# Scores of every second key tile in two borrowed banks, weight conversions in pairs, and a new order on every engine

## Chip, core and metric

The kernel runs on one core of one Trainium2 chip. The metric is the device time of one execution in microseconds; the figure given for a kernel is the median of its timed runs. The core has TensorE (PE) for matrix products, VectorE (DVE), ScalarE (ACT) and GpSimd (POOL) for elementwise work, SyncE (SP), which issues all the DMA transfers here, and 16 DMA engines. PSUM has 8 banks of 128 x 512 fp32.

## The reference

Block-sparse attention of 4 batches x 8 heads, 768 positions and head size 64, and behind it a feed-forward layer of 3072 tokens, 512 to 2048 to 512, with `h - tanh(h)` between:

```python
scores = scale * np.matmul(q, k.transpose(0, 1, 3, 2))
...
scores = np.where(mask, scores, -1000000000.0)
scores = scores - np.max(scores, axis=-1, keepdims=True)
attn = np.exp(scores)
attn = attn / (np.sum(attn, axis=-1, keepdims=True) + 1e-09)
return np.matmul(attn, v).astype(np.float32)
...
h = x @ w_in
g = h - np.tanh(h)
return (g @ w_out).astype(np.float32)
```

The mask lets each block of 32 queries see its neighbours, the first and last block and three sampled blocks.

## The kernel before

**Tiles and steps.** Heads come in pairs that are loaded together (`load_qk`, `load_v`). Queries and keys are split into a high part (`high`, ACT, L333) and a low part (`low`, L339), which are copied by DMA (`dist`, L362) into the slab: slots A and B for the maxima and the first half of the scores, C and D for the cross terms. The mask rides along as extra rows of A and B (`fill`). A step is one head and two of its six key tiles, so there are 96 steps, three per head. In step s, for key tile x of 0 and 1:

- `scores(s, x)`: four matmuls (L488, L489) into `pst`, 128 keys x 768 queries, two banks
- `expo(s, x)`: ACT's exponential (L492) from `pst` to `pe`
- `p_high` (ACT, L498) and `p_low` (POOL, L507): P as the sum of two fp16 parts, `ph` and `pl`
- `accum(s)`: 36 matmuls (L521, L524, L525) of P with V into `pav`

The maximum of each query row has to be known before its scores are exponentiated. It is found two heads ahead: `smax` (L455) writes score tiles to `psm` (three banks), `maxima` (DVE, L461) reduces two of them, `turn_max`, `neg_max` (L473) and `put_max` (a DMA of 3 KB, L479) put the row into slot B. V gets a scale (`v_max` L417, `v_all` L425, `v_scale` L429) and two fp16 parts (`v_high` L438, `v_low` L442). `norm` divides, `spill` writes the result out.

**Banks.** `pst` 2, `psm` 3, `pav` 1, and the two feed-forward banks `bank0` and `bank1`. In the first 28 steps these two serve only the start and the conversion of eight weight tiles: a tile is staged (`stage_w`), put together from its 64-bit words by three DVE operations (`convert`, L751, L755, L759) in a bank, and split into a high part (`res_hi`, ACT, L815) and a low part (`res_lo`, DVE, L819). `WSTEP` gives the step of each.

**Feed-forward.** From step 28 on pieces of four token chunks are worked on between the steps (`h_part` L854, `g_part`, `o_part`). What remains comes behind the last step: all its PE products are of 512 columns. Behind the attention its PSUM tiles are given to the feed-forward (`pf`).

**Order.** Each operation is added to a plan with a due time, an engine, a duration, and what it reads and writes. Sorted by due time, the operations of each engine are then taken in the order that the table `ORDER` says: each character is how many places ahead in the list of what is left the next one stands. So the due times and the table together fix one order for each engine, and an engine never leaves it. From durations and hops the plan works out a start for each operation; these starts set in which order the program text is emitted, and the count of fillers: `KeepBusy` puts small products of ones into `pav` (L240) where PE's plan has a gap.

Of the kernel before, what the change touches and what calls it, by code (L numbers as in the profile page):

```python
# [11 lines left out]
F32 = mybir.dt.float32  # L12
F32R = mybir.dt.float32r
F16 = mybir.dt.float16
# [30 lines left out]
        "#$$#'##$#############$##$#&$$###(%$###$#%$###$#$$$#$#%##'###%%%#&###%%$##%##$$##%##$$###%%###%#&$%$###&&###$#%"
        "#$#%$#######$######$##$#&$$$$###$##########'##$###$########'''#&#$##%&$$##&&#(%'#&*$###&'%%#&&#$$#%$%'##%%$#'&"
        ")%$&&#(##&#(#%$#$$&##$#&%%'##%%$#$$%$&#&%'#$&#$$#%#$''#$#$##%&#$&$%###$$''$$&##&*'#%$%##'$%($###$('#$$###$$('$"
        "$&#&&*#$#%$##'&$#''#*$#%&##('##)%($#%$#&#%$&#%($'#%#$#$%##'%$&$'#$##'$#)##&%##'###(%$$'(##%)#&&$'##&$)'#%'#(#$"
        "$#%'#'%$##%)&#%'#$#%%)(#$)###&*$#'$&$#'$%#'#&#)#'###''#)%($&#$('%%#%#%#$#%%$$(&#$'##&#$#'$'#$###$$'#%)$#&###%#"
        "#$(%#%$#'#*$'%##%##&%##$$$#$#%#$$##"  # L50
    ),
    "ACT": (
        "###$##$$$%$&%&%#,##%##$&#$#0#%##$#$#%3##$#$#$#$#$#$#%##$#$#,###$#$#1$#$#$#$#$#'#####%##,%$%$##%$#########'##$#"
        "####$####%$#$#%$%$%$%$%$%###$$$##$#%##$##$#$#$#$%$#$&#$#%##&#$#$#$*####%##$#%$#%$%$#$#$$#'##$$$#($#%$#%$%#####"
        "$#$#2#'#%$##$#$$$#&$$###%$%$###$#$#$#$#$#'#%###$#$$#&$#####$###$#$$$#$&#$####$#&#$#$##(#%###$#%$#%##%$#$#))##'"
        "#*$#(##$#$%$###%####$#$4#$$###$###$#$$#%#$$##$%$#$#$###$#####$#%##+#%#######'&$$#$#$#$$###%$$#1%#%####&%#%##($"
# [1096 lines left out]
```

## Time and profile before

| | us |
|---|---|
| median of 3 timed runs | 922.56 (921.46 to 923.68) |
| profiled execution | 921.18 |
| its span, first to last instruction | 919.4 |
| PE busy | 895.2 (97%) |
| DVE busy | 701.5 (76%) |
| ACT busy | 654.0 (71%) |
| POOL busy | 485.4 (53%) |

The busy shares are means over two very different parts. The attention, with pieces of feed-forward in it, lasts to about 463 us; behind it is feed-forward alone. PE's busy time is modelled (matmuls are pipelined) and in the early part holds the fillers. "Releaser" or "<-" in a row names what ended an engine's idle time.

### The profile page before, as it was taken

The page shows a single profiled execution, that of the slowest core. Times are in us where ns is not written, and L with a number is a line of the kernel's source. Part 1 is how long each engine was busy: PE and PEld are TensorE (multiplying, and loading weights), DVE is VectorE, ACT ScalarE, POOL GpSimd, SP SyncE. Part 2 cuts the span into 40 slices and gives each one's busy share as a digit, 9 for nine tenths or more (in the row PEclk, how much of TensorE's full clock was granted, in tenths as well). Part 3 has the DMA queues.
Part 4 walks back from the last instruction along what each step waited for, and adds up shares of the span by engine and source line. Part 5 has one row for each costly group of instructions (what it writes and reads, how often), then busy time and mean ns, then how long its engine had stood idle before and what let it go on. Part 6 is the DMA issues. An engine that isn't in the chain of part 4 may idle for free.

```text
span 919.4 us, 18275 instructions
## 1 busy us (share of the span) xinstructions
PE 895.2 (97%) x7177; PEld 744.8 (81%) x7177; DVE 701.5 (76%) x1000; ACT 654.0 (71%) x964; POOL 485.4 (53%) x324
## 2 busy tenths in 40 slices
PE   8998999999999999999989999999999999999998
PEld 4777778888887888888878888888888888888886
DVE  6987878889887888886469999985667666765765
ACT  5888888988889798798865666665555555555553
POOL 5677887778777676778842434532212222222131
PEclk9999999999999999999999999999999999999999
DMA  8878588766878758465352333230014202300201
GB/s 228 205 187 240 133 219 225 206 174 178 208 233 193 199 134 278 109 168 178 94 162 92 104 92 94 90 115 1 1 70 155 86 24 92 127 23 1 92 1 46
DMA packets 57677, 120.73 MB, mean 131 GB/s; under 512 B 6170, under 2 KB 26836, under 8 KB 56568
## 3 DMA queue, kind: packets, MB, share of 16 engines
q1 hardware_dynamic: 57592, 119.58, 45.5%
q8 instruction: 56, 0.92, 0.4%
q14 instruction: 29, 0.24, 0.1%
HBM read 55.68 MB, written 26.21 MB: 89 GB/s over the span
## 4 chain that ended last, share of the span: by engine, by line
PE 84%; ACT 6%; DVE 4%; DMA 3%; issue 2%; SPq 1%; POOL 0%; ACTq 0%; DVEq 0%
PE bank L854 27%; PE pf L889 8%; PE pf L891 8%; PE pf L890 8%; PE pst L488 7%; PE pst L489 6%; PE psm L455 5%; PE pav L521 3%; PE pav L524 3%; PE pav L525 3%; ACT pe L492 3%; PE bank L889 1%; DMA raw<-qk 1%; PE bank L890 1%; PE bank L891 1%
## 5 line engine op out<-in xcount | busy, mean ns | idle before, releaser
L507 POOL TENSOR_TENSOR pl<-pe,ph 128x768 f16<-128x768 f32 x192 | 320.4, 1688 | 95.4 <-ACT ph L498 49.8
L884 POOL TENSOR_TENSOR gl<-t,gh 128x512 fp32r<-128x512 f32 x96 | 126.9, 1323 | 298.6 <-ACT gh L882 233.3
L492 ACT ACTIVATE pe<-pst 128x768 f32<-128x768 f32 x192 | 155.2, 808 | 54.1 <-PE pst L489 52.1
L461 DVE TENSOR_REDUCE mc<-psm 128x2 f32<-128x1536 f32 x93 | 163.0, 1753 | 30.5 <-PE psm L455 29.8
L498 ACT ACTIVATE ph<-pe 128x768 f16<-128x768 f32 x192 | 157.9, 840 | 2.7 <-PE pav L525 0.3
L488 PE MATMUL pst<-slab 128*128 128x512 f32 (+1 forms) x384 | 141.6, 369 | 8.7 <-ACT pe L492 7.4
L868 DVE TENSOR_TENSOR t<-t,bank 128x512 f32<-128x512 f32 x96 | 65.7, 684 | 94.3 <-ACT t L866 69.0
L489 PE MATMUL pst<-slab 97*128 97x512 f32 (+1 forms) x384 | 122.4, 340 | 0.0
L521 PE MATMUL pav<-vhl,ph 128*128 128x65 f16 x1152 | 116.4, 194 | 0.1
L524 PE MATMUL pav<-vhl,ph 128*128 128x64 f16 x1152 | 115.8, 195 | 0.0
L525 PE MATMUL pav<-vhl,pl 128*128 128x65 f16 x1152 | 115.3, 192 | 0.0
L521 PEld LDWEIGHTS <-ph 128*128 128x128 f16 x1152 | 105.5, 96 | 7.0 <-issue 4.4
L874 ACT ACTIVATE u<-u,bias 128x512 f32<-128x512 f32 x96 | 69.2, 721 | 58.3 <-DVE bank L876 57.8
L524 PEld LDWEIGHTS <-ph 128*128 128x128 f16 x1152 | 106.6, 97 | 0.4 <-issue 0.2
L525 PEld LDWEIGHTS <-pl 128*128 128x128 f16 x1152 | 106.7, 99 | 0.0
L488 PEld LDWEIGHTS pst<-slab 128*128 128x128 f32 x384 | 72.6, 189 | 32.0 <-ACT pe L492 19.7
L455 PE MATMUL psm<-slab 88*128 88x512 f32 (+1 forms) x378 | 87.9, 350 | 5.9 <-DVE nm L473 1.9
L866 ACT ACTIVATE t<-bank 128x512 f32<-128x512 f32 x96 | 56.7, 591 | 43.5 <-PE bank L854 38.8
L864 ACT ACTIVATE u<-bank 128x512 f32<-128x512 f32 x96 | 57.0, 594 | 43.0 <-PE bank L854 41.8
L882 ACT ACTIVATE gh<-t 128x512 fp32r<-128x512 f32 x96 | 60.3, 628 | 36.3 <-DVE t L880 18.1
L880 DVE COPY_PREDICATED t<-u,bank 128x512 f32<-128x512 int32 x96 | 71.5, 745 | 18.9 <-ACT u L874 13.5
L890 PE MATMUL pf<-wx,gh 128*128 128x512 f32 x216 | 84.1, 389 | 0.0
(135 smaller groups left out, 1918.5 us busy)
## 6 DMA issues: line engine op xcount, KB each, us to landing
slab<-hm SPq DMA_DIRECT2D x124, 192.0 KB
slab<-lo SPq DMA_DIRECT2D x63, 192.0 KB
raw<-qk SPq DMA_DIRECT2D x15, 768.0 KB
stage<-w_in SPq DMA_DIRECT2D x16, 512.0 KB
stage<-w_out SPq DMA_DIRECT2D x16, 512.0 KB
xsav<-xbuf SPq DMA_DIRECT2D x4, 2048.0 KB
rawv<-v SPq DMA_DIRECT2D x16, 384.0 KB
xscr<-xq SPq DMA_DIRECT2D x16, 384.0 KB
```

The costliest lines, as they stand in the source:

```text
L455: nc.tensor.matmul(o[:, b0 + c0 : b0 + c1], lhsT=sB[s][0:88, t * P : (t + 1) * P], rhs=sA[s][0:88, c0:c1], start=True, stop=True)
L461: nc.vector.tensor_reduce(out=mcs[h][:, t - 1 : t + 1], in_=psm.rearrange("p (x s) -> p x s", x=2), op=ALU.max, axis=AX.X)
L488: nc.tensor.matmul(pst[:, q], lhsT=sC[c][:, kc], rhs=sD[c][:, q], start=True, stop=False)
L489: nc.tensor.matmul(pst[:, q], lhsT=sA[a][0:97, kc], rhs=sB[a][0:97, q], start=False, stop=True)
L492: nc.scalar.activation(out=pe[s % 2][:, x * S : (x + 1) * S], in_=pst[:, 0:S], func=AF.Exp, scale=0.125)
L498: nc.scalar.activation(out=phs[s][0][:, c], in_=pe[s % 2][:, c], func=AF.Copy)
L507: eng.tensor_tensor(out=pl[:, c], in0=pe[s % 2][:, c], in1=ph[:, c], op=ALU.subtract)
L521: nc.tensor.matmul(oav[:, t, :], lhsT=ph[:, c], rhs=vv[:, 0:65], start=(kt == 0 and t == 0), stop=False, skip_group_check=True)
L524: nc.tensor.matmul(oav[:, t, 0:64], lhsT=ph[:, c], rhs=vv[:, 65:129], start=False, stop=False, skip_group_check=True)
L525: nc.tensor.matmul(oav[:, t, :], lhsT=pl[:, c], rhs=vv[:, 0:65], start=False, stop=last, skip_group_check=True)
L854: self.nc.tensor.matmul(h, lhsT=w[:, cc], rhs=z[:, c, :], start=(c == 0 and x == 0), stop=(c == NCT - 1 and x == 2))
L890: self.nc.tensor.matmul(o, lhsT=gh[:, c], rhs=wo[1][ft], start=False, stop=False)
```

## The change

The scores of key tile 1 go to the feed-forward banks in the steps of `TWICE`, 18 of the steps 1 to 26: columns 0 to 511 to `bank0`, 512 to 767 to `bank1`. Each part is an operation of its own in the plan, and so is its exponential, so that a step then has three exponentials. The last two steps of each six are left out, and in these the weight tiles are converted, now two at a time, one in each bank (`WSTEP`). The halves `ph` and `pl` of P now lie in one tile, key tile by key tile. The table `FULL` (key tiles whose P would stay fp32) is empty, so the functions `v_full` and `whole` are not used; two memsets of `vf` are added. The plan's durations and hops are other numbers. All five rows of `ORDER` are new.

```diff
+FULL = {}
+TWICE = [s for s in range(1, 27) if s % 6 not in (4, 5)]
-WSTEP = (2, 5, 8, 11, 14, 17, 20, 23)
+WSTEP = (4, 4, 10, 10, 16, 16, 22, 22)
...
-    HOP = {"PE": 0.045, "ACT": 0.08, "DVE": 0.03, "POOL": 0.1, "SP": 0.03}
+    HOP = {"PE": 0.045, "ACT": 0.1, "DVE": 0.05, "POOL": 0.11, "SP": 0.03}
...
+    def score_area(s, x, q):
+
+        if q is None:
+            return pst, ((0, 512), (512, S))
+        return ffn.hb[q], (((0, 512), (512, S))[q],)
+
+    def scores(s, x, q=None):
         h, i = divmod(s, 3)
         a, c = h % 4, h % 2
         kc = slice((2 * i + x) * P, (2 * i + x + 1) * P)
-        for q in (slice(0, 512), slice(512, S)):
-            nc.tensor.matmul(pst[:, q], lhsT=sC[c][:, kc], rhs=sD[c][:, q], start=True, stop=False)
-            nc.tensor.matmul(pst[:, q], lhsT=sA[a][0:97, kc], rhs=sB[a][0:97, q], start=False, stop=True)
+        area, parts = score_area(s, x, q)
+        for c0, c1 in parts:
+            o = area[:, c0 - parts[0][0] : c1 - parts[0][0]]
+            nc.tensor.matmul(o, lhsT=sC[c][:, kc], rhs=sD[c][:, c0:c1], start=True, stop=False)
+            nc.tensor.matmul(o, lhsT=sA[a][0:97, kc], rhs=sB[a][0:97, c0:c1], start=False, stop=True)
+
+    def expo(s, x, q=None):
+        o = whole(s, x) if full(s, x) else pe[s % 2][:, x * S : (x + 1) * S]
+        area, parts = score_area(s, x, q)
+        c0, c1 = parts[0][0], parts[-1][1]
+        nc.scalar.activation(out=o[:, c0:c1], in_=area[:, 0 : c1 - c0], func=AF.Exp, scale=0.125)
...
-            for n, k in enumerate((0.038, 0.039, 1.038)):
+            for n, k in enumerate((0.038, 0.039, 0.5)):
...
-            add(s + 1.08, "ACT", act(512), self.res_hi, (m, ft, bank[j]), [("bank", j)], [("w", m, 0, ft)])
-            add(s + 2.038, "DVE", dve(512), self.res_lo, (m, ft, bank[j]), [("bank", j), ("w", m, 0, ft)], [("w", m, 1, ft)])
+            add(s + 0.6, "ACT", act(512), self.res_hi, (m, ft, bank[j]), [("bank", j)], [("w", m, 0, ft)])
+            add(s + 1.5, "DVE", dve(512), self.res_lo, (m, ft, bank[j]), [("bank", j), ("w", m, 0, ft)], [("w", m, 1, ft)])
...
-        "#$%&#&'########(((##&####%%##########%##&#*##(##*&##&*#%##%###&%##$'#%##($#%###&#####&###'###############$#%##"
+        "#$%&#&'########+((-##'*##$'####&&###$%###%###%####&&##$&'#%%##%%%)(###*##(%####%##%##$#####$#%##%#####%#$&$#&(%"
```

The operations are the same in number on every engine but for ACT (984 for 966), DVE (two memsets) and the fillers of PE (81 for 94).

SP, the transfers around the load of heads 2 and 3 (`raw1`) before; `slab<-slab` and `slab<-lo0` are the two copies `first_dist`, `slab<-pe` the masks, `slab<-hm` and `slab<-lo` other copies to the slab, `slab<-nm` a row of maxima:

```order
L358 DMA slab_80<-slab_80 64x768
L401 DMA slab_80<-pe0_164 32x768 x2
L401 DMA slab_80<-pe1_165 33x768 x3
L362 DMA slab_80<-hm0_216 64x768
L358 DMA slab_80<-lo0_212 64x768
L362 DMA slab_80<-hm0_216 64x768
L327 DMA rawv0_242<-v 128x768
L741 DMA stage0_81<-w_in 128x4x256
L745 DMA stage1_82<-w_out 128x1024
L317 DMA raw1_267<-qk 128x1536
L362 DMA slab_80<-lo0_212 64x768 x2
L317 DMA raw2_285<-qk 128x1536
```

The same place now:

```order
L333 DMA rawv0_190<-v 128x768
L407 DMA slab_80<-pe0_168 32x768
L364 DMA slab_80<-slab_80 64x768
L364 DMA slab_80<-lo0_218 64x768
L368 DMA slab_80<-hm0_220 64x768 x2
L407 DMA slab_80<-pe1_169 33x768
L803 DMA stage1_82<-w_out 128x1024
L323 DMA raw1_264<-qk 128x1536
L368 DMA slab_80<-lo0_218 64x768 x2
L407 DMA slab_80<-pe1_169 33x768
L368 DMA slab_80<-hm0_220 64x768
L407 DMA slab_80<-pe1_169 33x768
```

Now `rawv0` stands ahead of both copies `first_dist`; only w_out is left between them and `raw1`. The load of the next pair, `raw2`, was the third transfer behind `raw1`, right ahead of the copies of `hm1`; it is no longer in this piece. SP seven transfers on, now:

```order
L368 DMA slab_80<-hm1_313 64x768 x2
L368 DMA slab_80<-hm0_220 64x768
L503 DMA slab_80<-nm1_371 1x6x128
L799 DMA stage0_81<-w_in 128x4x256
L333 DMA rawv1_394<-v 128x768
L368 DMA slab_80<-hm1_313 64x768 x3
L323 DMA raw2_414<-qk 128x1536
L368 DMA slab_80<-lo1_374 64x768
L323 DMA raw3_431<-qk 128x1536
```

The staging of w_in and the loads of `raw2` and `raw3` stand behind the row `nm1` and the first copies of `hm1`.

ACT in steps 14 and 15 before (`pe0` and `pe1` are P of even and odd steps, `ph14` and `ph15` its high parts):

```order
L492 ACTIVATE pe0_164<-pst_154 128x768
L333 ACTIVATE hm4_1273<-raw4_1082 128x1536
L492 ACTIVATE pe1_165<-pst_154 128x768
L498 ACTIVATE ph14_1224<-pe0_164 128x768
L492 ACTIVATE pe1_165<-pst_154 128x768
L498 ACTIVATE ph15_1341<-pe1_165 128x768
L492 ACTIVATE pe0_164<-pst_154 128x768
L498 ACTIVATE ph16_1359<-pe0_164 128x768
```

The same steps now:

```order
L527 ACTIVATE pe0_168<-pst_154 128x768
L527 ACTIVATE pe1_169<-bank1_79 128x256
L527 ACTIVATE pe0_168<-bank0_78 128x512
L531 ACTIVATE ph13_1139<-pe1_169 128x768
L339 ACTIVATE hm4_1200<-raw4_793 128x1536
L527 ACTIVATE pe1_169<-pst_154 128x768
L527 ACTIVATE pe0_168<-bank1_79 128x256
L531 ACTIVATE ph14_1226<-pe0_168 128x768
L527 ACTIVATE pe1_169<-bank0_78 128x512
L531 ACTIVATE ph14_1226<-pe0_168 128x768
L527 ACTIVATE pe1_169<-bank1_79 128x256
L531 ACTIVATE ph15_1281<-pe1_169 128x768
```

Before, every exponential reads `pst`, and the two of step 15 have other work between them. Now there are three for each of steps 14 and 15, those of key tile 1 from `bank0` and `bank1`, and step 15's first one from `pst` comes before the last part of step 14.

DVE between the maxima of heads 5 and 6 (`mc5`, `mc6`) before, with the conversions L751, L755, L759 and the low parts L819:

```order
L461 TENSOR_REDUCE mc5_907<-psm_155 128x2
L755 SCALAR_TENSOR_TENSOR bank0_78<-stage0_81,bank0_78 128x512
L759 SCALAR_TENSOR_TENSOR bank0_78<-stage0_81,bank0_78 128x512
L473 TENSOR_SCALAR nm5_1122<-psm_155 6x128
L819 TENSOR_TENSOR wi12_138<-bank0_78,wi02_137 128x512
L819 TENSOR_TENSOR wo11_136<-bank1_79,wo01_135 128x512
L461 TENSOR_REDUCE mc6_1127<-psm_155 128x2
L751 TENSOR_SCALAR bank1_79<-stage1_82 128x512
L461 TENSOR_REDUCE mc6_1127<-psm_155 128x2
```

The same place now (L809, L813 and L817 are the conversions, L877 the low parts):

```order
L817 SCALAR_TENSOR_TENSOR bank0_78<-stage0_81,bank0_78 128x512
L817 SCALAR_TENSOR_TENSOR bank1_79<-stage1_82,bank1_79 128x512
L485 TENSOR_REDUCE mc5_871<-psm_155 128x2
L448 SCALAR_TENSOR_TENSOR vhl0_157<-rawv2_716,sb2_938,vhl0_157 128x12x64
L574 SCALAR_TENSOR_TENSOR rs2_1003<-pav_156,sb1_567 128x6
L577 RECIPROCAL rs2_1003<-rs2_1003 128x6
L578 TENSOR_TENSOR xq1_1002<-pav_156,rs2_1003 128x6x64
L485 TENSOR_REDUCE mc5_871<-psm_155 128x2
L877 TENSOR_TENSOR wi11_134<-bank0_78,wi01_133 128x512
L497 TENSOR_SCALAR nm5_1064<-psm_155 6x128
L877 TENSOR_TENSOR wo11_136<-bank1_79,wo01_135 128x512
L485 TENSOR_REDUCE mc6_1073<-psm_155 128x2 x2
```

Before, the conversion of the next tile begins in `bank1` between the maxima of head 6; now both banks are converted and split side by side within the maxima of head 5, and those of head 6 follow without a conversion between them.

## Rows read from the trace of the kernel before

**Rows 1.** Busy time of each engine by stretches of the span: stretch and its length, then for each engine busy us and the count of instructions, the granted clock of PE, the busy share of the DMA engines and their GB/s.

```profile
0.00:14.00 14.00, 11.86 (x46) 6.15 (x47) 8.51 (x21) 6.73 (x9) 7.83 (x12) 1.00 0.72 174
14.00:46.00 32.00, 29.37 (x309) 22.16 (x308) 28.12 (x36) 25.58 (x32) 20.92 (x13) 1.00 0.87 234
46.00:138.00 92.00, 84.69 (x1080) 70.07 (x1079) 75.99 (x96) 79.27 (x100) 72.75 (x43) 1.00 0.75 195
138.00:463.00 325.00, 319.24 (x3748) 276.56 (x3748) 257.96 (x343) 280.15 (x383) 247.67 (x152) 1.00 0.67 185
463.00:483.00 20.00, 17.59 (x96) 13.55 (x93) 13.36 (x24) 13.36 (x23) 8.87 (x7) 1.00 0.44 138
483.00:897.00 414.00, 413.79 (x1829) 341.28 (x1828) 305.52 (x466) 241.55 (x407) 123.51 (x96) 1.00 0.21 70
```

The order of the engines in a row is PE, PE's weight loads, DVE, ACT, POOL.

**Rows 2.** Waits from 46 to 138 us, all engines: who waited for whom, us in total, times, longest.

```profile
ACT pe L492 <- PE pst L489: 13.1, 36, 1.3
PEld pst L488 <- ACT pe L492: 10.4, 20, 1.2
...
POOL pl L507 <- ACT ph L498: 5.1, 10, 1.6
PE pst L488 <- ACT pe L492: 4.5, 12, 1.0
```

**Rows 3.** ACT in order of time from 57 us on: start us, duration us, line, operation, and in brackets the idle time before it and its releaser.

```profile
57.79 0.81 ACT L492 ACTIVATE pe<-pst 128x768 f32<-128x768 f32 x1 [0.25 <-PE pst L489]
58.50 1.48 ACT L333 ACTIVATE hm<-raw 128x1536 fp32r<-128x1536 f32 x1
...
62.40 0.81 ACT L492 ACTIVATE pe<-pst 128x768 f32<-128x768 f32 x1 [0.25 <-PE pst L489]
...
64.34 0.81 ACT L492 ACTIVATE pe<-pst 128x768 f32<-128x768 f32 x1 [0.25 <-PE pst L489]
```

**Rows 4.** The chain that ended last, from 10 to 36 us: start us, us, what.

```profile
13.49 8.61 DMA raw<-qk
...
24.13 4.58 DMA slab<-hm
...
28.85 0.95 PE psm L455 x4
```

**Rows 5.** ACT in order of time again, exponentials of the ramp and the first ones of steps 6 and 28.

```profile
20.34 0.81 ACT L492 ACTIVATE pe<-pst 128x768 f32<-128x768 f32 x1 [0.19 <-PE pst L489]
...
25.17 0.81 ACT L492 ACTIVATE pe<-pst 128x768 f32<-128x768 f32 x1 [0.24 <-PE pst L489]
...
31.32 0.79 ACT L492 ACTIVATE pe<-pst 128x768 f32<-128x768 f32 x1
...
45.82 0.81 ACT L492 ACTIVATE pe<-pst 128x768 f32<-128x768 f32 x1 [1.28 <-PE pst L489]
...
137.68 0.81 ACT L492 ACTIVATE pe<-pst 128x768 f32<-128x768 f32 x1
```

**Rows 6.** Busy time by stretches within the ramp, columns as in rows 1.

```profile
12.00:22.00 10.00, 8.99 (x46) 6.06 (x44) 7.35 (x9) 6.92 (x9) 7.71 (x5) 1.00 1.00 304
22.00:29.00 7.00, 5.65 (x57) 3.53 (x57) 6.62 (x9) 6.57 (x8) 1.33 (x1) 1.00 0.82 223
```

**Rows 7.** Transfers issued by SP in the first 14 us: what, count, KB each. (The tile of w_out has the size of that of w_in.)

```profile
raw<-qk SPq DMA_DIRECT2D x1, 768.0 KB
stage<-w_in SPq DMA_DIRECT2D x1, 512.0 KB
...
rawv<-v SPq DMA_DIRECT2D x1, 384.0 KB
slab<-pe SPq DMA_DIRECT2D x3, 99.0 KB
...
slab<-lo SPq DMA_DIRECT2D x1, 192.0 KB
```

**Rows 8.** Groups of ACT's instructions by line and shape: line, out<-in, shapes and count, busy us, mean ns of one, idle us before them and releasers. L492 is the exponential, L864 reads a feed-forward bank.

```profile
L492 ACT ACTIVATE pe<-pst 128x768 f32<-128x768 f32 x192 | 155.2, 808 | 54.1 <-PE pst L489 52.1 <-POOL pl L507 0.7 <-DMA stage<-w_out 0.2
...
L864 ACT ACTIVATE u<-bank 128x512 f32<-128x512 f32 x96 | 57.0, 594 | 43.0 <-PE bank L854 41.8 <-DVE t L868 0.2
```

**Rows 9.** Groups of DVE's instructions from 46 to 138 us: the conversions and the low parts of the weights.

```profile
L755 DVE SCALAR_TENSOR_TENSOR bank<-stage,bank 128x512 int32<-128x512 int32 x5 | 3.4, 685 | 0.0
L759 DVE SCALAR_TENSOR_TENSOR bank<-stage,bank 128x512 int32<-128x512 int32 x5 | 3.4, 683 | 0.0
L751 DVE TENSOR_SCALAR bank<-stage 128x512 int32<-128x512 int32 x4 | 2.7, 681 | 0.0
...
L819 DVE TENSOR_TENSOR wi<-bank,wi 128x512 fp32r<-128x512 f32 x3 | 2.1, 684 | 1.1 <-ACT wi L815 1.1
L819 DVE TENSOR_TENSOR wo<-bank,wo 128x512 fp32r<-128x512 f32 x3 | 2.0, 682 | 0.1
```

**Rows 10.** Waits from 138 to 463 us, columns as in rows 2.

```profile
ACT pe L492 <- PE pst L489: 36.4, 58, 2.6
POOL pl L507 <- ACT ph L498: 36.2, 25, 5.0
```

**Rows 11.** PE in order of time where the last attention product ends, columns as in rows 3.

```profile
463.31 3.01 PE L854 MATMUL bank<-xbuf,wi 128*128 128x512 f32 x12
...
468.31 2.56 PE L854 MATMUL bank<-xbuf,slab 128*128 128x512 f32 x10 [1.54 <-POOL slab L928]
471.25 3.06 PE L854 MATMUL bank<-xbuf,slab 128*128 128x512 f32 x12 [0.38 <-DVE t L880]
```

More of the change, by code (lines that the diff above doesn't have):

```diff
@@ L45 @@
[L45 to L49, printed above, removed]
@@ L207, in order @@
                 if e == "PE":
-                    d += 0.09 * (not o[10] and (fp16 or t > free[e] + 0.02))
-                    fp16 = o[10]
+                    d += 0.085 if kind == 2 else 0.09 * (not o[10] and (kind or t > free[e] + 0.02))
+                    kind = int(o[10])
                 free[e] = t + d
@@ L215, in order @@
                 same = ops[j][2] == e and e != "SP"
-                ready[j] = max(ready[j], free[e] if same else end + self.HOP[ops[j][2]])
+                k = end + 0.03 if (i, j) in reads else free[e]
+                ready[j] = max(ready[j], k if same else end + self.HOP[ops[j][2]])
                 left[j] -= 1
@@ L305, in attention @@
     vhl = [acst.tile([P, 2, T, 129], F16, name=f"vhl{i}") for i in range(NV)]
+    vf = [acst.tile([P, 2, 2, 65], F32, name=f"vf{i}") for i in range(NV)]
     for i in range(NV):
         nc.vector.memset(vhl[i][:, :, :, 64:65], 1.0)
+        nc.vector.memset(vf[i][:, :, :, 64:65], 1.0)
     sl = ffn.slab.rearrange("p (n s) -> p n s", s=S)
@@ L444, in v_low, with full, v_full, halves @@
         )
-    mcs, nms, phs, xq = {}, {}, {}, {}
+    def full(s, x):
+        return 2 * (s % 3) + x in FULL.get(s // 6, ())
+    def v_full(pr):
+        kts = FULL[pr]
+        t = slice(kts[0], kts[-1] + 1, max(1, kts[-1] - kts[0]))
+        vv = rawv[pr].rearrange("p (h t) d -> p h t d", h=2)[:, :, t]
+        nc.scalar.activation(out=vf[pr % NV][:, :, 0 : len(kts), 0:64], in_=vv, func=AF.Copy, scale=sbs[pr])
+    mcs, nms, phs, xq = {}, {}, {}, {}
+    def halves(s):
+        if s not in phs:
+            phs[s] = p2.tile([P, 2, 2, S], F16, tag="ph", name=f"ph{s}", bufs=3)
+        return phs[s]
+    def whole(s, x):
+        return halves(s).bitcast(F32)[:, x].rearrange("p y c -> p (y c)")
     def smax(h, t, o=None):
@@ L552, in at @@
             xs = (0, 1) if isinstance(x, slice) else (x,)
-            dur, w = 1.07 * len(xs), [("raw", pr % 2, i) for i in xs]
+            dur, w = 1.65 * len(xs), [("raw", pr % 2, i) for i in xs]
         elif n == "load_v":
-            dur, w = 1.07, [("rawv",)]
+            dur, w = 1.7, [("rawv",)]
         elif n == "high":
@@ L624, in at @@
         elif n == "spill":
-            dur, r, w = 1.3, [("xq", args[0] % 2, x) for x in range(2)], [("xscr", args[0] // 4)]
-        add(due, eng, dur, f, args, r, w, **kw)
+            dur, r, w = 1.8, [("xq", args[0] % 2, x) for x in range(2)], [("xscr", args[0] // 4)]
+        add(due, eng, dur, f, args, r, w, **({"half": 2} if n in ("turn_max", "v_all") else kw))
     AB = ((sA, 0, hms, 0), (sB, 0, hms, 1))
@@ L725, in attention @@
         for x in range(2):
-            at(s + (0.01, 0.065)[x], scores, s, x)
-            at(s + (0.02, 0.067)[x], expo, s, x)
-            at(s + (0.068, 1.03)[x], p_high, s, x)
-            at(s + (0.069, 1.04)[x], p_low, s, x)
+            for q in (0, 1) if x and s in TWICE else (None,):
+                a = (s, x) if q is None else (s, x, q)
+                k = 0.0 if q is None else 0.0001 * q - 0.03
+                at(s + (0.01, 0.065)[x] + k, scores, *a)
+                at(s + (0.02, 0.067)[x] + k, expo, *a)
+            if not full(s, x):
+                at(s + (0.068, 1.03)[x], p_high, s, x)
+                at(s + (0.069, 1.04)[x], p_low, s, x)
         at(s + 2.09, accum, s)
```

189 lines of the change are left out of this document (106 added, 83 removed).

## The prediction, made before the changed kernel was run

> **What bounds the kernel now.** I read the stretches first [rows 1]. From 483 to 897 us TensorE is busy 413.79 of 414 us: there the other engines only feed it, and the operations are the same in both kernels. The tail behind the last attention product (463.31 us [rows 11] to the end) can therefore change only where it starts and where it ends. From 46 to 138 us no engine is full: ACT 79.27 of 92 us, VectorE 75.99, GpSimd 72.75. TensorE's 84.69 there are modelled and hold fillers. The clock column says 1.00 in each of these stretches.
>
> So I looked at the attention part for waits [rows 2]. From 46 to 138 us the largest of ACT's waits is for a score tile: 13.1 us in 36 pieces. The reverse wait, TensorE for ACT's exponential, is 10.4 us on its weight loads and 4.5 us on its matmuls; these lie partly on top of each other and are not added. It is one loop: there is one score tile, pst, and it is written, read, written again. Its round shows in ACT's timeline [rows 3]: from the exponential at 62.40 to the one at 64.34 are 1.94 us, two of them 3.88 us, one step of two key tiles. From the first exponential of step 6 at 45.82 to that of step 28 at 137.68 [rows 5] are 22 steps, 4.18 us each: the round of pst plus 0.3.
>
> Then I read the ramp by the chain of waits [rows 4]. From 13.49 to 22.1 us the chain is one transfer, raw<-qk, the keys and queries of heads 2 and 3. Behind it come its high part, a weight part (L815), 4.58 us of copies slab<-hm, and at 28.85 us the score maxima of head 2. TensorE's order has the scores of step 3 behind these, so step 3 waits too: ACT's exponentials stand at 20.34, 25.17 and, two further on, 31.32 us [rows 5], where the round of pst alone would put them 1.94 us apart. The DMA engines are full from 12 to 22 us, at 304 GB/s [rows 6]. What stands right ahead of raw<-qk in SP's queue is rawv, w_in and w_out, 384, 512 and 512 KB [rows 7].
>
> **The ramp.** The new order of SP moves rawv ahead of first_dist0 and first_dist1, into a time when the engines are not full (share 0.72 to 14 us [rows 1]), takes w_in behind the row put_max1, and puts the second raw<-qk (768 KB, ahead of the copies before) far behind them. Ahead of the first raw<-qk 384 + 512 = 896 KB go: 896 KB / 304 GB/s = 2.9 us. Between it and the copies of head 2 stood two lo copies (384 KB) and the second raw<-qk, 1152 KB; now two lo, one hm and two masks, 774 KB: 378 KB less, 1.2 us. Sum 4.1 us, which everything behind the maxima of head 2 gets, since step 3 stands behind them. Bounds: nothing, if rawv, now ahead of first_dist0, delays step 0 by as much as it gives; and 13.2 us of the two DMA pieces [rows 4] less 960 KB / 304 = 3.2 us, so 10 us at most. I take 4.1, the row that tells the rate.
>
> The Trainium skill ("DMA: Bandwidth & Descriptors", Queues, rings and completion order) says that each DMA engine takes the descriptors of a ring in order. By that rule the 896 KB count in full, and the trace agrees: 384 + 512 + 512 + 768 KB at 304 GB/s are 7.2 of the 8.6 us. If instead all transfers in flight shared the engines, the first raw<-qk would gain less, and the term would be nearer 1.2 than 4.1.
>
> **Two more banks for scores.** In 18 steps (1 to 26 without the last two of each six) the scores of the second key tile go to the two feed-forward banks, so TensorE can write them while ACT still reads pst. The columns are the same. ACT reads them by two exponentials, of 512 and of 256 columns. A 512-column read of a bank takes 594 ns, the 768-column exponential 808 ns [rows 8]: 0.836 ns a column, hence about 380 ns for 256. Two together 974 ns, 166 ns more than one. Fifteen of the 18 steps lie between 46 and 138 us: 15 x 0.166 = 2.5 us more on ACT.
>
> What goes: in 15 of the 22 steps the waits of ACT for scores. 13.1 x 15 / 22 = 8.9 us; I let two thirds go, 6.0, since the first key tile still has pst alone and the two steps of conversions keep the old round. Less 2.5: 3.5 us gain. What is late next is VectorE: it idles 92 - 75.99 = 16 us in this stretch, which is the end on the good side; 2.5 us of loss, no wait removed and nothing hidden, is the other. I keep to the value near the wait row. A start distance in rows 3 (57.79 to 58.50) says that an exponential holds ACT some 0.1 us less than its duration, so ACT has room for the split.
>
> **Conversions in pairs.** Eight weight tiles are converted in steps 4, 4, 10, 10 and so on, two at once, before one each three steps. Nothing is added: each has three conversions and a low part on VectorE, at 0.68 to 0.69 us [rows 9]. A pair is 8 x 0.69 = 5.5 us in one place where 2.7 us were. In the order of VectorE they lie between the maxima of two heads. I cost it at nothing: VectorE's 16 idle us cover it. If that cover is missing, see the third rival.
>
> **Order elsewhere.** Fillers fall from 94 to 81; they run while TensorE has nothing else, so nothing. From 138 to 463 us TensorE is busy 319.24 of 325 us [rows 1]. The operations there are the same; an ideal order gives 5.8 us, a worse one could cost as much (an estimate from the same row, its idle time doubled). I take 2 us of gain: ACT waits 36.4 and GpSimd 36.2 us there [rows 10], and not all of that is hidden. In the change of phase TensorE waits 1.54 us for a split of weights and once 0.38 us for VectorE [rows 11]; the new order puts a second product and a transpose between the two units there: 1 us, bounds 2.4 both ways (20 - 17.59 [rows 1]). The two memsets and the layout of the halves of P move nothing.
>
> **Sum.** 4.1 + 3.5 + 2 + 1 = 10.6 us. The profiled execution took 921.18 us, 919.4 of it span; the change is all inside the span, so it would take 910.6. The median of the three timed runs is 922.56, 1.4 us above the profiled one; so a median of 912.0. The likeliest case by itself spans 906 to 917.
>
> **Rivals.**
> *Only the ramp.* The banks give nothing, because VectorE (75.99 of 92) or GpSimd (72.75) holds the step at 4.18 us; the split is hidden in ACT's idle time. For it: GpSimd's own waits there, in L507, name ACT in 5.1 us only. Against: the many short waits on pst. 922.56 - 4.1 = 918.5.
> *The gain is caught up.* The steps start earlier, but the stretch after 138 us is TensorE's (319.24 of 325) and the new order loses there what the ramp and the banks gave, 7.6 us: 922.6, no change. Against: that stretch would have to grow by 2.3% with the same work.
> *Slower: pairs at the banks.* The scores of the second tile may be written to the banks only after the low parts of both weights, and TensorE works in order, so accumulations, maxima and first scores queue behind. VectorE's load there without conversions and low parts (20 of them, 13.6 us [rows 9]) is 75.99 - 13.6 = 62.4 us, 2.84 a step. Two steps of 4.18 leave 2.7 us, a pair needs 5.5: 2.8 us late, four times 11.2 us. With no gain from banks and 4.1 from the ramp: 922.56 + 11.2 - 4.1 = 929.7. It decides from the point where the first second-tile scores after a pair wait over 2 us for L877.
> *The clock.* Fewer fillers stand in the ramp's waits. In 14 to 46 us TensorE is busy 29.37 us at the 2.4 GHz level; a fall to 1.2 GHz for the time of the transfers (12 to 29 us, some 14.6 us busy [rows 6]) doubles that work, mostly into waits; if all of it showed, 912 + 14.6 = 926.6. Against: the granted clock is 1.00 throughout. The Trainium skill ("TensorE: Matmul & The Clock Gate", Why this matters for your kernels) warns that idle gaps between bursts bring the half clock back; in this trace waits of 1.5 us did not.
> *More than I ask.* All waits on pst go (13 us less 2.5), ramp 6, the rest 4: 922.56 - 20.5 = 902.
>
> **How the numbers follow.** The forecast 0.50, only the ramp 0.15, more 0.10, caught up 0.10, pairs 0.12, clock 0.03. The measurement tells 0.2%, 1.85 us, from no change, so 920.7 to 924.4 is the same. Faster: 0.50 + 0.15 + 0.10 and 0.03 of the caught-up case, 0.78; same 0.05 of it; slower 0.02 of it, 0.12 and 0.03, 0.17. The range reaches from 901, the end of the better case, to 923, which holds most of the caught-up case; outside are the slower ones and a little below.
>
> **What would show it.** In the profile after: raw<-qk should land at about 19 us and the maxima of head 2 start at about 24.5 us; the first exponential of step 28 at about 130 us in place of 137.68 [rows 5]; ACT's wait for scores between the ramp's end and step 27 at half of 13.1 us or less; the last accumulation at about 454 in place of 463.3; from there to the end 455 us as before. If the maxima of head 2 still start after 28 us, the ramp is wrong; if the steps from 6 to 27 still last 4.18 us, the banks are; if TensorE waits for L877, the pairs decide.

## The result and the profile after

The change makes the kernel slower: 927.2 us (median of 8 runs) against 921.12 us for the kernel before (8 runs beside them), ratio 1.006, 95% interval 1.0043 to 1.0078. One of the eight executions of the changed kernel took 3078.51 us; the ratio is that of the other seven, whose median is 926.58. 912.0 had been forecast, with 901 to 923 as the range: the direction was wrong, and the time lies outside the range. The profiled execution took 928.28 us, its span is 926.5 us, against 919.4.

The stretches of [rows 1], for the changed kernel (stretch, length; busy us and count of PE, its weight loads, DVE, ACT, POOL; granted clock; DMA share, GB/s):

```profile
0.00:14.00 14.00, 11.86 (x45) 6.13 (x46) 9.48 (x24) 6.47 (x9) 7.90 (x12) 1.00 0.72 185
14.00:46.00 32.00, 28.55 (x315) 23.07 (x314) 27.37 (x34) 26.29 (x38) 21.19 (x13) 1.00 0.86 235
46.00:138.00 92.00, 86.70 (x1168) 74.43 (x1167) 81.84 (x106) 82.75 (x122) 78.94 (x46) 1.00 0.78 203
138.00:463.00 325.00, 316.54 (x3667) 274.71 (x3665) 254.62 (x342) 277.09 (x382) 248.07 (x152) 0.99 0.66 185
463.00:483.00 20.00, 18.13 (x77) 14.83 (x78) 12.67 (x19) 10.07 (x18) 4.39 (x4) 0.83 0.26 84
483.00:897.00 414.00, 410.40 (x1788) 331.92 (x1787) 296.27 (x456) 236.42 (x396) 120.69 (x94) 1.00 0.21 70
```

From 46 to 138 us every engine does more than before. The loss is in the last two rows. The clock falls below 1.00 at the change of phase, and from 483 to 897 us TensorE runs 1788 products in place of 1829. PE's busy column hides most of that (410.40 against 413.79), because a matmul's end is modelled. The count does not: 41 products at the usual distance of 0.227 us between starts are 9.3 us. Nor does the column of the weight loads: 331.92 against 341.28 us.

**Up to step 28 the attention part came out as forecast.** I follow it by ACT's exponentials. In order of time (start us, duration us, line, operation): the high part of the first raw<-qk, the last exponentials of steps 3 and 8, the first of step 28:

```profile
19.45 1.48 ACT L339 ACTIVATE hm<-raw 128x1536 fp32r<-128x1536 f32 x1
...
28.41 0.81 ACT L527 ACTIVATE pe<-pst 128x768 f32<-128x768 f32 x1
...
52.09 0.38 ACT L527 ACTIVATE pe<-bank 128x256 f32<-128x256 f32 x1
...
129.94 0.80 ACT L527 ACTIVATE pe<-pst 128x768 f32<-128x768 f32 x1
```

Step 28 begins 7.7 us earlier than before [rows 5]. VectorE's first maxima of head 2, here and then in the kernel before:

```profile
26.93 1.76 DVE L485 TENSOR_REDUCE mc<-psm 128x2 f32<-128x1536 f32 x1 [1.53 <-PE psm L479]
```

```profile
29.82 1.76 DVE L461 TENSOR_REDUCE mc<-psm 128x2 f32<-128x1536 f32 x1 [0.79 <-PE psm L455]
```

The waits from 46 to 138 us, as in [rows 2]:

```profile
ACT pe L527 <- PE pst L521: 4.6, 9, 1.5
...
PEld pst L520 <- ACT pe L527: 3.7, 7, 1.2
...
ACT pe L527 <- PE bank L521: 2.1, 4, 0.9
```

ACT's waits for score tiles are 6.7 us where they were 13.1. The low parts of the paired conversions (L877) are waited for by TensorE twice before 463 us, 0.5 us in all. The last accumulation ends at 457.6 us (454 forecast), before at 463.5.

**The tail is longer.** From the end of the last accumulation to the start of TensorE's last instruction are 464.7 us, before 451.8: 12.9 us more for the same operations. The first part of it is the change of phase. TensorE there (in brackets the idle time before and its releaser):

```profile
457.42 2.99 PE L912 MATMUL bank<-xbuf,wi 128*128 128x512 f32 x12
460.25 0.61 PE L912 MATMUL bank<-xbuf,slab 128*128 128x512 f32 x2
464.87 4.64 PE L912 MATMUL bank<-xbuf,slab 128*128 128x512 f32 x10 [4.00 <-POOL slab L986]
```

POOL at that time, and the stretches around it:

```profile
459.85 4.96 POOL L986 TENSOR_TENSOR slab<-slab 128x512 fp32r<-128x512 f32 x4
```

```profile
460.00:465.00 5.00, 1.00 (x5) 0.51 (x3) 3.13 (x5) 2.93 (x5) 4.81 (x4) 0.92 0.98 288
465.00:470.00 5.00, 5.00 (x12) 3.94 (x13) 0.28 (x1) 1.03 (x2) 1.28 (x1) 0.50 0.15 52
```

TensorE waits 4.00 us, in [rows 11] it was 1.54, until the last of GpSimd's four splits; then the clock stands at 1.2 GHz, and ten products take 4.64 us that took 2.56.

The second part is spread out. Waits from 490 to 897 us, in the changed kernel and then in the one before (L880 there is L938 here, the copy_predicated that frees the bank of a unit):

```profile
PEld bank L912 <- DVE t L938: 12.3, 25, 1.1
...
PE bank L912 <- DVE t L938: 3.3, 10, 0.7
```

```profile
PEld bank L854 <- DVE t L880: 1.7, 4, 0.6
...
PE bank L854 <- DVE t L880: 0.2, 1, 0.2
```

Taken from the starts of TensorE's products (every distance over 0.27 us, less 0.227), the pauses between 490 and 895 us are 9.6 us, before 1.7. This is the number that the expectations below use.

### The profile page after: what moved, and what is told of

It reads as the page before. It is cut to its first block, busy times and chain, and to the rows that moved or that the text cites. A ratio compares the mean times of both kernels' runs of the same rounds, so it can differ in the third digit from the quotient of the medians.

```text
span 926.5 us, 18295 instructions
## 1 busy us (share of the span) xinstructions
PE 897.9 (97%) x7164; PEld 745.9 (81%) x7164; DVE 699.6 (76%) x1002; ACT 651.8 (70%) x982; POOL 487.6 (53%) x324
## 5 line engine op out<-in xcount | busy, mean ns | idle before, releaser
L540 POOL TENSOR_TENSOR ph<-pe,ph 128x768 f16<-128x768 f32 x192 | 324.9, 1713 | 95.4 <-ACT ph L531 48.8
L942 POOL TENSOR_TENSOR gl<-t,gh 128x512 fp32r<-128x512 f32 x96 | 124.7, 1302 | 312.9 <-ACT gh L940 271.4
L527 ACT ACTIVATE pe<-pst 128x768 f32<-128x768 f32 x174 | 140.7, 808 | 42.5 <-PE pst L521 40.1
L926 DVE TENSOR_TENSOR t<-t,bank 128x512 f32<-128x512 f32 x96 | 65.6, 685 | 106.1 <-ACT t L924 66.9
L520 PE MATMUL pst<-slab 128*128 128x512 f32 x348 | 126.7, 364 | 6.9 <-ACT pe L527 6.7
L563 PE MATMUL pav<-vhl,ph 128*128 128x65 f16 x1152 | 117.0, 194 | 0.3 <-DVE xq L578 0.2
L567 PE MATMUL pav<-vhl,ph 128*128 128x65 f16 x1152 | 115.8, 193 | 0.0
L521 PE MATMUL pst<-slab 97*128 97x512 f32 x348 | 111.7, 342 | 0.0
L563 PEld LDWEIGHTS <-ph 128*128 128x128 f16 x1152 | 105.7, 97 | 6.8 <-issue 3.2
L566 PEld LDWEIGHTS <-ph 128*128 128x128 f16 x1152 | 107.1, 97 | 0.5 <-issue 0.5
L567 PEld LDWEIGHTS <-ph 128*128 128x128 f16 x1152 | 107.1, 99 | 0.0
L948 PE MATMUL pf<-wx,gh 128*128 128x512 f32 x240 | 93.4, 389 | 0.0
L947 PE MATMUL pf<-wx,gh 128*128 128x512 f32 x240 | 93.4, 389 | 0.0
L949 PE MATMUL pf<-wx,gl 128*128 128x512 f32 x240 | 93.4, 389 | 0.0
L924 ACT ACTIVATE t<-bank 128x512 f32<-128x512 f32 x96 | 56.7, 592 | 43.5 <-PE bank L912 39.1
L520 PEld LDWEIGHTS pst<-slab 128*128 128x128 f32 x348 | 66.3, 191 | 23.1 <-ACT pe L527 12.1
```

Of the source, the lines that this page charges most:

```text
L520: nc.tensor.matmul(o, lhsT=sC[c][:, kc], rhs=sD[c][:, c0:c1], start=True, stop=False)
L527: nc.scalar.activation(out=o[:, c0:c1], in_=area[:, 0 : c1 - c0], func=AF.Exp, scale=0.125)
L540: eng.tensor_tensor(out=pl, in0=pe[s % 2][:, c], in1=ph, op=ALU.subtract)
L563: nc.tensor.matmul(oav[:, t, :], lhsT=ph[:, c], rhs=vv[:, 0:65], start=(kt == 0 and t == 0), stop=False, skip_group_check=True)
L566: nc.tensor.matmul(oav[:, t, 0:64], lhsT=ph[:, c], rhs=vv[:, 65:129], start=False, stop=False, skip_group_check=True)
L567: nc.tensor.matmul(oav[:, t, :], lhsT=pl[:, c], rhs=vv[:, 0:65], start=False, stop=last, skip_group_check=True)
```

## The experiments

All twelve ran beside the kernel before; the ratio is to that. "Tail" is counted as above, from the one execution of each that was profiled. Edits of an order are written out as steps of the plan; in the kernel they are marks of `ORDER`.

| edit | us | before, beside it | ratio, 95% interval | tail, us |
|---|---|---|---|---|
| the change itself | 927.2 | 921.12 | 1.006 (1.0043 to 1.0078) | 464.7 |
| splits in order of need | 922.61 | 921.49 | 1.0013 (0.9992 to 1.0034) | 460.5 |
| old order of the tail | 919.15 | 921.49 | 0.9963 (0.9943 to 0.9984) | 455.0 |
| new tail on the kernel before | 932.11 | 921.49 | 1.0095 (1.0072 to 1.0118) | 461.1 |
| weight loads later | 923.72 | 921.49 | 1.0019 (1.0001 to 1.0037) | 463.3 |
| the three together | 914.58 | 922.18 | 0.9915 (0.9893 to 0.9937) | 451.6 |
| units in turn on VectorE | 924.54 | 922.18 | 1.0037 (1.0023 to 1.0052) | 463.6 |
| new splits on the kernel before | 928.19 | 922.18 | 1.0067 (1.0048 to 1.0086) | 457.8 |
| fillers in the wait | 924.74 | 922.18 | 1.0029 (1.0008 to 1.005) | 461.9 |
| fewer twin steps | 942.26 | 922.35 | 1.0202 (1.0176 to 1.0229) | 464.7 |
| light first pair | 926.39 | 922.35 | 1.0026 (1.0006 to 1.0046) | 463.4 |
| units in turn and more room | 927.11 | 920.19 | 1.0078 (1.0059 to 1.0097) | 463.3 |
| the three, and fillers in the ramp | 912.65 | 920.19 | 0.9922 (0.9899 to 0.9945) | 451.7 |

**Splits in order of need.** GpSimd's `split_w`, four marks of its table:

```diff
-split_w i 5, split_w o 4, split_w o 5, split_w i 4
+split_w i 4, split_w i 5, split_w o 4, split_w o 5
```

> The changed kernel; only GpSimd's order of the four splits of weights at the change of phase is turned: input weights 4 first, then 5, then the output weights (it was 5, output 4, output 5, input 4). Theory (the stall is the order of the splits): TensorE's first unit there needs input weights 4, which come out as the fourth of four splits of 1.28 us. As the first, its wait of 4.0 us falls to under 0.5, the granted clock does not fall to 0.5 from 465 to 470 us, and what that cost (4.64 us for ten products in place of 2.56, and two to three more) goes too: 6 to 7 us, about 921. Rival (the wait is for the weights' arrival or for ACT's part): the wait stays above 3 us and the time at 927. Second rival (the wait moves): the next unit waits for input weights 5 or the transposes instead, the gap is cut in two and 2 us at most are gained.

```profile
456.24 2.56 PE L912 MATMUL bank<-xbuf,slab 128*128 128x512 f32 x10 [0.33 <-POOL slab L986]
```

The wait is 0.33 us, the clock stays at 1.00, the products take 2.56 us. The tail is 4.2 us shorter and the time 4.3 by the ratios, less than the 6 to 7 expected: behind these products TensorE now meets the transposes too early and waits 0.86, 0.21 and 0.75 us there. So the rival of a moved wait holds in part.

**New splits on the kernel before**, the same edit backwards.

```diff
-split_w o 4, split_w i 4, split_w i 5, split_w o 5
+split_w i 5, split_w o 4, split_w o 5, split_w i 4
```

> The kernel before; only GpSimd's order of the four splits is that of the changed kernel (input 5, output 4, output 5, input 4). Theory (order of the splits, and the clock behind the pause): TensorE's wait of 1.54 us at 468 us grows by two splits of 1.28 us to about 4.1; behind it the granted clock is 0.5 for some 5 us, which costs 2.5 more: 921.5 + 5 = 926.5. Rival (wait without the clock): 924. Rival (there is slack behind it): 921.5.

```profile
475.56 8.10 PE L854 MATMUL bank<-xbuf,slab 128*128 128x512 f32 x22 [6.33 <-POOL slab L928]
```

```profile
475.00:480.00 5.00, 4.44 (x11) 3.48 (x12) 0.00 (x0) 0.00 (x0) 1.74 (x2) 0.50 0.02 7
```

6.0 us slower, and the tail is longer by just that, though a little more than the 5 expected. The wait is even longer than computed, since GpSimd's first split there waits 2.31 us for ACT's high part of input 5, which is third in ACT's old order. Four marks in the table of an engine that is busy 53% of the time cost 6 us.

**Fillers in the wait** take the wait and its clock apart.

```diff
+        for _ in range(18):
+            nc.tensor.matmul(pav[:, 0:512], lhsT=ones[:, 0:P], rhs=ones[:, 0:512], start=True, stop=True, skip_group_check=True)
     with ExitStack() as fctx:
```

> The changed kernel with 18 products of 512 columns put into TensorE's order at the change of phase, ahead of the unit that waits for the fourth split; they write an accumulator that nobody reads any more. The wait itself stays. Theory (the clock falls because TensorE paused 4 us): the fillers take the pause, the granted clock stays at 1.00 from 460 to 475 us, the ten products behind it take 2.6 us and not 4.64, and the time is 2.5 to 3 us less, about 924.5. Rival (the clock falls for another reason, or the modelled end hides that nothing was slower): 927. If the fillers run longer than the pause, up to 1 us is lost.

```profile
457.19 4.06 PE L295 MATMUL pav<-ones 128*128 128x512 f16 x18
460.90 3.47 PE L914 MATMUL bank<-xbuf,slab 128*128 128x512 f32 x12
```

The clock is 1.00 in every stretch from 455 to 475 us, the tail 2.8 us shorter. The intervals of the two times overlap, so the size rests on the tails: of what the order of the splits cost, some 3 us were the clock behind the pause. The Trainium skill ("TensorE: Matmul & The Clock Gate", Why this matters for your kernels) warns of idle gaps that bring the half clock back; the trace agrees: 0.50 behind 4.00 us of pause, 1.00 behind the 1.54 us of [rows 11].

**Old order of the tail, and the new one on the kernel before.** Only the marks of the steps behind the attention change places, on all five engines.

> The changed kernel, but behind the attention every engine's order of the feed-forward part (416 steps of TensorE, 432 of ACT, 496 of VectorE, 100 of GpSimd, 74 of SP) is that of the kernel before; the attention part and the splits stay as changed. Theory (the searched order of the tail makes TensorE wait for VectorE's copy_predicated): the pauses of TensorE between 490 and 895 us, 9.6 us in the changed kernel and 1.7 in the one before, go back to about 2, so 927.2 - 8 = 919; the stall at 460 us with its low clock stays. Rival (these pauses come from something earlier, the low clock or transfers that the new attention part has shifted): they stay, 927.

> The kernel before, with the changed kernel's order of the feed-forward part behind the attention on all engines; attention and the order of the splits stay as before. Theory (order of the tail): the pauses between 490 and 895 us rise from 1.7 to 8 to 10 us, so about 921 + 8 = 929, slower than the changed kernel although its attention is the old one. Rival (the attention part spoils the tail): no change, 921.

The first, from 483 to 897 us:

```profile
483.00:897.00 414.00, 413.79 (x1829) 341.23 (x1828) 305.67 (x466) 242.10 (x409) 123.61 (x97) 1.00 0.21 69
```

Busy time and count of TensorE are those of [rows 1], and the pauses are 1.5 us. The second has pauses of 10.0 us, the changed kernel's picture with the old attention:

```profile
PEld bank L854 <- DVE t L880: 12.7, 25, 1.1
```

Both tails moved by 9.3 to 9.7 us: the order of these steps is the cause, not what stands ahead of it. The version with the old tail is already faster than the kernel before.

**Units in turn.** Why is the bank late? One place in the changed kernel, VectorE:

```profile
586.32 0.68 DVE L926 TENSOR_TENSOR t<-t,bank 128x512 f32<-128x512 f32 x1
589.67 0.69 DVE L926 TENSOR_TENSOR t<-t,bank 128x512 f32<-128x512 f32 x1 [2.68 <-ACT u L922]
590.28 1.29 DVE L928 TENSOR_TENSOR bank<-bank,u 128x512 f32<-128x512 f32 x2
591.60 0.69 DVE L934 SCALAR_TENSOR_TENSOR bank<-u,bank 128x512 f32<-128x512 f32 x1
592.33 0.69 DVE L936 SCALAR_TENSOR_TENSOR bank<-qq,bank 128x512 f32<-128x512 f32 x1
592.94 0.69 DVE L809 TENSOR_SCALAR pf<-stage 128x512 int32<-128x512 int32 x1
593.53 0.74 DVE L938 COPY_PREDICATED t<-u,bank 128x512 f32<-128x512 int32 x1
```

The two L926 belong to two units. The second's stands ahead of the first's last four steps, and waits, by way of ACT's L922, for products that TensorE ends only at 588.46; the first's copy comes at 593.53, and TensorE starts its next unit at 594.42. In VectorE's order a unit's first step stands ahead of the copy of the unit before in 31 of 80 places, in the kernel before in 19. By the records the time from a unit's last product to the end of its copy is 7.6 us in the median, before 6.6, while the room that TensorE leaves between two uses of a bank is nearly the same (8.4 and 8.2 us).

```diff
 DVE, where it can stand so (24 of 31 places), u and v two units one after the other
-g_part u 2, g_part v 2, g_part v 3, g_part u 3, g_part u 6, g_part u 7, g_part u 8
+g_part u 2, g_part u 3, g_part u 6, g_part u 7, g_part u 8, g_part v 2, g_part v 3
```

> The changed kernel; only VectorE's order behind the attention is edited: where a unit's first two steps stood ahead of the last step (the copy that frees the bank) of the unit before, they are moved right behind it, in 24 of 31 places; TensorE, ACT, GpSimd and SP keep the changed order. Theory (VectorE serves the next unit first, so the bank comes free late): the time from a unit's last product to its copy, 7.6 us in the median against 6.6 in the kernel before, goes down by 0.5 to 1, TensorE's pauses between 490 and 895 us fall from 9.6 to 4 to 6, the time to about 922.5. Rival (TensorE's own order leaves too little room between two uses of a bank): nothing changes, 927. Second rival (ACT's order sets the chain): the copy comes as late as it did, VectorE only waits elsewhere, 926 to 928.

The time is 0.2% nearer to the kernel before, though its interval overlaps that of the change. The copy comes after 7.1 us, half of the difference; but the pauses fall only to 8.2 us, outside what was expected. VectorE's service order is at most a small part.

**Units in turn and more room** adds an edit of TensorE's order.

```diff
 PE, 17 moves, until six products second stand between h_part u and the next use of its bank
-h_part u, second, second, h_part v, second, second, h_part w
+h_part u, second, second, h_part v, second, second, second, second, h_part w
```

> The changed kernel with two edits of the order behind the attention: VectorE serves the units in turn in 24 places, as in the run before, and on TensorE at least six second products stand between two units that use the same bank (17 moves; there were places with three or four). Theory (the pauses come where the chain to the copy, 7.1 us by the median of that run, meets too little room): TensorE's pauses between 490 and 895 us fall from 8.2 us with the first edit alone to 5 to 6, the time from 924.5 to about 922. Rival (places with little room are not what costs; the chain is late where room is plenty, by ACT's order too): pauses stay at 8, 924 to 925.

The theory falls: pauses of 9.8 us, 927.11. The least room between two uses of a bank rose from 5.1 to 6.8 us, so places with little room are not what costs. What the traces show besides is more units that are late: between 490 and 890 us, 21 of 72 units of the changed kernel need over 8.5 us from the last product to the end of the copy, 19 of 71 here, 8 of 73 in the kernel before. In the changed kernel the two longest pauses at such a place (0.87 and 0.73 us) stand behind units that took 10.3 and 10.9 us. Which engine's order makes them late stays open: no run exchanges the order of one engine alone.

**Weight loads later.** The attention part has a third loss. ACT and TensorE of the changed kernel, step 37:

```profile
176.68 1.48 ACT L339 ACTIVATE hm<-raw 128x1536 fp32r<-128x1536 f32 x1 [4.25 <-issue]
```

```profile
178.92 0.79 PE L520 MATMUL pst<-slab 128*128 128x512 f32 x1 [3.90 <-ACT pe L527]
```

The high part may overwrite hm only when the copies of head 13 have read it, and SP issues two weight loads of 512 KB at 164.70 and 166.19, ahead of these. The clock is 0.50 from 178 to 184 us.

```diff
 SP
-stage_w o 4, put_max 13, stage_w i 4, dist 13, dist 13, dist 15
+put_max 13, dist 13, dist 13, stage_w o 4, stage_w i 4, dist 15
```

> The changed kernel; only in SP's queue the two loads of weights (output 4 and input 4, 512 KB each) at 165 us are moved behind the last two copies of head 13, which the next high part on ACT must await. Theory (copies behind bulk loads): ACT's idle 4.2 us before that high part at 176.7 us shrink to under 1.5, TensorE's wait of 3.9 us at 174.9 goes with it, the clock does not fall to 0.5 from 178 to 184 us; 4 + 2.5 = 6 us, about 921, if the steps behind keep it. Rival (caught up): the steps behind are bound by something else and the last accumulation ends where it did, 927. Second rival (the high part waits for its load, not for the copies): nothing moves at 172 us.

```profile
172.82 1.48 ACT L339 ACTIVATE hm<-raw 128x1536 fp32r<-128x1536 f32 x1
```

The wait is gone and the clock stays at 1.00 there; 3.5 us, not 6. SP issues the two copies at nearly the same time as before the edit (166.51 and 167.03 us, before 166.66 and 167.21), so it is what stands ahead of them in the queue. The size was taken from one execution: in five others of the same attention order ACT waits 1.9 to 2.6 us there, in one 3.9. From the first exponential of step 28 to the end of the last accumulation this version takes 321.7 us, the changed kernel 327.6, its five variants above 323.1 to 325.2, the kernel before 325.8. The Trainium skill ("DMA: Bandwidth & Descriptors", Queues, rings and completion order) has each engine take a ring's descriptors in order; the vanished wait agrees (4.25 us, then none).

**Fewer twin steps.**

```diff
-TWICE = [s for s in range(1, 27) if s % 6 not in (4, 5)]
+TWICE = [1, 2, 3, 7, 8, 9, 26]
```

> The changed kernel with 11 of the 18 twin steps (6, 12 to 15, 18 to 21, 24 and 25) back to one score area: their second key tile is written to pst and read by one exponential of 768 columns; every order is otherwise that of the changed kernel. Theory (the banks are worth more than predicted): from the accumulation of step 8 to that of step 28 the kernel before takes 85.5 us, the changed one 75.8 to 77.3 in the executions seen, 8 to 10 us for 15 twin steps, some 0.6 us each; 11 steps back cost 6 to 7 us there, ACT's waits for score tiles between 46 and 138 us rise from 5.2 us to 9 or more, and the time is about 933. Rival (the predicted size, 3.5 us for 15 steps): 2.6 us, about 930. Second rival (that stretch is shorter because of the other new orders): no change, 927.

By the ratios some 13 us slower than the change, more than either theory. ACT's waits for pst from 46 to 138 us are 11.7 us (4.6 in the change), TensorE's for ACT 8.2 and 4.1 (3.7 and 1.7). The banks do remove the wait, but an order made for them is worse without them than the old one was, so this doesn't give their size. The accumulations used there misled too: in the new order they stand later behind their exponentials. By exponentials, from the end of step 8's last to the first of step 28, it is 81.0 us before and 77.5 now.

**Light first pair.**

```diff
+        if ft == 0:
+            convert_part(self.nc, n, self.raw[m, ft][:, 0:64], t[:, 0:32], c[:, 0:32])
+            return
         convert_part(self.nc, n, self.raw[m, ft], t, c)
```

(and the low part alike; the high part goes to a scratch tile, and memsets fill the rest)

> The changed kernel, in which VectorE converts only 32 of the 512 columns of the first pair of weight tiles (input 0 and output 0; the rest of them are zeros, so this part of the feed-forward result is left out): eight steps of 0.69 us become short, about 4.7 us less work on VectorE at steps 4 and 5. Theory (what the ramp gave is lost because VectorE is full behind it, 15.55 of 16 us from 30 to 46): the accumulation of step 8, at 62.0 us (63 to 64.5 in other executions of the same attention orders), comes 3 to 4 us earlier, and some of that reaches the end: 923 to 926. Rival (ACT or the later transfer of the second keys and queries holds the steps there): step 8 moves by less than 1 us, 927.

From 30 to 46 us VectorE (third pair of numbers) is busy 11.47 us in place of 15.55; this version, then the change:

```profile
30.00:46.00 16.00, 15.19 (x175) 12.73 (x175) 11.47 (x22) 13.83 (x19) 11.53 (x8) 0.90 0.84 217
```

```profile
30.00:46.00 16.00, 14.70 (x209) 12.21 (x208) 15.55 (x21) 13.69 (x19) 13.05 (x8) 1.00 0.87 228
```

The exponentials don't come closer: from the last of step 3 to the last of step 8 are 23.2 us in both. The theory falls: the first pair's conversions were hidden, though in this execution the clock was also low from 26 to 33 us. The other three pairs were not lightened; for them there is only the wait of 0.5 us above. The median doesn't tell, its interval touches that of the change.

**The three together**: splits, tail and weight loads.

> The changed kernel with the three edits together: the splits with input weights 4 first, the two loads of weights behind the copies of head 13, and the old order of the feed-forward part behind the attention. Theory (three separate losses): what the three gave one by one adds up, 4.6 + 3.5 + 8.0 us off 927.2, so 911 (909 to 914), faster than both kernels; TensorE's pauses are below 2 us each and the clock stays at 1.00. Rival (they overlap, for instance because the steps behind the attention's stall catch it up): 914 to 917, no better than the old tail alone by more than 2 to 5 us.

Faster than both kernels, 0.85% below the one before, though 3.6 us above the sum. The tail is 451.6 us, as before the change. The profiled execution lost time elsewhere, in the ramp: the high part behind raw<-qk starts 3.8 us later than in the change, with ACT idle for 3.91 us until that transfer, and the clock is at 0.50 from 28.1 to 34.9 us:

```profile
24.00:28.00 4.00, 0.98 (x4) 0.68 (x4) 1.76 (x1) 3.77 (x7) 2.47 (x1) 1.00 0.52 117
28.00:32.00 4.00, 3.40 (x10) 2.95 (x11) 1.75 (x1) 1.63 (x3) 1.68 (x2) 0.51 0.87 253
```

**The three, and fillers in the ramp.**

```diff
+                if ops[k][4].__name__ == "smax" and ops[k][5][:2] == (2, 0):
+                    for _ in range(30):
+                        nc.tensor.matmul(pav[:, 390:512], lhsT=ones[:, 0:P], rhs=ones[:, 390:512], start=False, stop=True, skip_group_check=True)
```

> The version with the three edits together, and 30 more fillers of 122 columns (1.7 us) on TensorE ahead of the first score maxima of head 2, where it waits for copies in the ramp; they write columns of the accumulator that nobody reads. Theory (in the executions where keys and queries land late, a pause there brings the clock to 0.5 for some 5 us, as seen in the profiled one of the three edits): the clock stays at 1.00 from 24 to 36 us and the median goes from 914.6 to about 913, with fewer executions above 915. Rival (the pause is longer than the fillers, or the cost is the late transfer itself): no difference, 914 to 915; if they delay the maxima, up to 1 us more.

The clock in the ramp is 1.00 in the execution profiled, but there the high part started at 19.86 us, so it isn't the late case that the fillers were meant for. The ratio, 0.9922, is that of the version without them (0.9915). Nothing to tell: one version or the other is the best of the study, and why the sum of the three falls short stays open.

## Why the prediction was wrong

- *The ramp, -4.1*: right in the mechanism, with 2.9 of the 4.1 us. The high part behind raw<-qk starts 2.7 us earlier (2.9 computed), VectorE's maxima of head 2 at 26.93 in place of 29.82; the 1.2 us more for the copies didn't come. That ACT is 4.2 us ahead by the end of step 8 (52.5 against 56.7) meets the number partly by luck: steps 3, 6, 7 and 8 have the two banks already.
- *Two banks, -3.5*: right in the sum, 81.0 - 77.5 = 3.5 us from step 8 to 28, and ACT's waits fell by 6.4 us (6.0 forecast). The first exponential of step 28, forecast at about 130, came at 129.94. How much of it the banks give and how much the new order of that stretch is not shown: the run with fewer twin steps doesn't tell. One execution of each is also thin: the same stretch took 83.2 us in both other runs with the old attention order, and 76.6 to 79.5 us in the others with the new one.
- *Pairs at nothing*: right, by the light pair for the first of them and by TensorE's waits for L877, at most 0.3 us where the rival asked for over 2; so the slower rival on which most of that side's chance lay was the wrong one.
- *Order elsewhere, -2*: missed in the profiled execution. From step 28 to the last accumulation the change lost 1.9 us (327.6 against 325.8), because a wait behind weight loads at 175 us ate the gain; with the loads moved it is 321.7, a gain of 4.1. In five other executions of the same attention order the gain was 0.6 to 2.7 us, in one (the light pair) 2.6 us were lost.
- *Transition, -1*: wrong sign, and outside its bounds of 2.4 us. I read TensorE's order only. The wait in [rows 11] was one for GpSimd, whose four splits the change turned so that the needed one comes last. Measured: 4.2 us lost, and 6.0 when the same order is put on the kernel before.
- *"The tail can therefore change only where it starts and where it ends"*: this is the step that failed. It took a stretch with TensorE busy 413.79 of 414 us for one that an order can't touch. The diff replaces the order of every step in it, on five engines. A stretch that is full has nothing to win by that and all of its cover to lose; no rival named this. Measured: 9.3 to 9.7 us, shown both ways. That the new order is the cause is shown; by which of its steps is not.
- *Clock* (3% of the chance): in the changed kernel's ramp it stayed at 1.00 with fewer fillers. That it falls with pauses was right in other places: between 459 and 479 us in each execution in which TensorE stood still until the fourth split, near 180 us in some. In other executions of the new attention order it fell in the ramp too.

Sum for the profiled spans: -7.7 to step 28, +1.9 to the last accumulation, +12.9 in the tail, 7.1 us, as measured.

## What to carry to other kernels

When a change searches all orders anew, read the full stretches first: there a new order can only lose. Exchange old and new order there before the search is trusted, and look at the order of the engine that releases each wait, not of the one that waits. Keep the two halves of such a change apart: here the early half won 5.8 us in the profiled executions and the late half lost 12.9; with the late half put back and the two weight loads moved, the whole is 7.6 us faster than the kernel before. Follow pace by the instruction that sets it, and a saturated engine by its count of instructions, not by its busy share.

## What the runs showed of the hardware

Nine times, in eight executions, TensorE stood still for 3.90 us, 3.99 to 4.01 us or 6.33 us without fillers, and each time the granted clock fell to 0.50; the ten products after one of these pauses took 4.64 us for 2.56. 18 products that nobody reads kept the clock at 1.00 in one such place, and the tail was 2.8 us shorter. The length of the pause alone doesn't decide: at the same place of the order the clock had fallen with a pause of 1.86 us (old tail, at 177.74 us) and had not with one of 2.21 us (fillers in the wait, at 178.00 us). The landing of one and the same transfer differs between executions: the high part behind raw<-qk started between 19.2 and 23.2 us in those of the new attention order, in the latest after 3.91 us of idle time for that transfer, so one profile sizes such a wait badly.
